# A decode block with its gradients: two weight gradients stored in blocks of 120 and 32 rows from another queue, and the side work in another order

## The chip, the cores and the metric

The kernel runs on one core of a Trainium2 chip. The metric is the device time of one execution in microseconds. The kernel before takes 1714.44 us, the median of three runs (1713.85 to 1715.55). The profiled execution spans 1712.4 us from its first to its last instruction.

## What is computed

A transformer block for one decode step, forward and backward. The batch is B = 4, the width D = 512, there are H = 32 heads of Dh = 128, the cache has Sk = 4096 rows, and the inner width of the feed-forward part is F = 1792. All data are bf16.

```python
def attn(x, K, V, wq, wo):                     # x: (4, 1, 512); K, V: (4, 32, 4096, 128)
    q = (x @ wq).reshape(B, 1, H, Dh).transpose(0, 2, 1, 3)
    p = softmax(einsum("bhqd,bhkd->bhqk", q, K) * Dh ** -0.5)
    o = einsum("bhqk,bhkd->bhqd", p, V)
    return o.transpose(0, 2, 1, 3).reshape(B, 1, H * Dh) @ wo

h  = x + attn(layernorm(x), K, V, wq, wo)
h2 = h + (silu(layernorm(h) @ w1) * (layernorm(h) @ w3)) @ w2

# returned: h2 and, for the given grad_out, the gradients of x, K, V, wq, wo, w1, w3, w2
```

The caches dominate. K and V hold 128 pairs of batch and head, 1 MB each; both are read, V is read a second time in the backward part, and the gradients of K and V, of the same size, are written. The gradients of wq (512 x 4096) and wo (4096 x 512) have 4 MB each, those of w1, w3 and w2 1.75 MB each.

## The kernel before

SBUF is cut into 23 slots of 128 partitions x 4160 bf16. A tile takes a slot, and gives it back when it has been used; who takes it next waits until the last reader is done, a store included.

The backward part goes through the 128 pairs, called heads here and in the code's index `s`. For each it loads V once more (a DMA issued by ACT), transposes it (TensorE and ACT), makes dP from it, and builds two outer products on VectorE, `gv` and `gk`, which are the gradients of V and K. The store of `gv` is issued by GpSimd, that of `gk` by SyncE.

```python
def grad_V(s):
    gv = Slot("gv")
    outer(gv.heads(), P2s.pop(s), reps["rdo", ...])          # VectorE
    nc.gpsimd.dma_start(out=rows_of(out_3[b, h]), in_=gv.heads())
    gv.give()

def grad_K(s):
    gk = Slot("gk")
    outer(gk.heads(), dS2s[s // B][:, s % B], reps["rq", ...])
    nc.sync.dma_start(out=rows_of(out_2[b, h]), in_=gk.heads())
    gk.give()
```

All else that the backward part has to do is a generator, `side_work`, whose units are run between the heads. A unit ends at a `yield`.

```python
def grad_unit(dst, lhsT, rhs):                   # one 128 x 512 piece of a weight gradient
    ps = psg.tile([P, 512], FP32)
    nc.tensor.matmul(ps[:, 0:n], lhsT=lhsT, rhs=rhs, start=True, stop=True)   # K = 4 rows
    grad_flush()                                 # ACT copies the piece before this one
    gu.append((dst, ps, n))

def side_work():
    ...
    for s in range(NH):                          # dq: 128 products in fp32, three to a unit
        nc.tensor.matmul(dq_ps[:, s:s + 1], lhsT=M_of(s)[:, 0:Dh], rhs=dOT_f[:, s:s + 1], ...)
        if s % MC == MC - 1:
            Ms[s // MC].give()
            if s // MC in (3, 5):
                load_wq2(s // MC // 2 - 1)       # wq once more, from SyncE
        if s % 3 == 2:
            yield
    ...                                          # dq to rows (dqflat)
    for cc in range(DC):                         # dx: wq transposed, 16 times 8 blocks, and multiplied
        for h0 in range(0, H, 8):
            ...                                  # 8 transposes
            yield
            nc.scalar.copy(out=wv[:, h0:h0 + 8, :], in_=pt[:])
        ...                                      # 3 more units
    ...                                          # layer norm backward, out_1
    for cc in range(DC):                         # gradient of wq: four blocks of 128 rows
        if cc == DC - 2:
            w2 = load_w2()
        st = Slot("gwq")
        for n8 in range(HD // 512):
            grad_unit(...)
            yield
        grad_flush()
        nc.gpsimd.dma_start(out=out_4[cc * P:(cc + 1) * P, :], in_=st.b(HD))
        st.give()
    ...                                          # rows for the feed-forward part, out_0
    ...                                          # gradient of w2 (14 units, 2 stores)
    ...                                          # oflat: the rows of O, by four small DMAs
    ...                                          # gradients of w1 and w3 (32 units, 4 stores)
    ...                                          # gradient of wo (32 units, 4 stores of 128 partitions)

for s in range(NH):                              # the loop over the heads
    load_ahead(s + L)
    ...
    front(s + L)                                 # V transposed, dP
    grad_V(s + LV)
    grad_K(s)
    ...
    if s >= S0:                                  # S0 = 21, L = 5, LV = 3
        step("s", 3 if s < S0 + 15 else 2)
    elif s >= O0:
        step("o")
step("s", 400)                                   # what is left
```

Of the kernel before, what the change touches and what calls it, by code (L numbers as in the profile page):

```python
# [24 lines left out]
def kernel(  # L25
# [22 lines left out]
    nc = tc.nc  # L48
    P = nc.NUM_PARTITIONS

    B = A_x.shape[0]
    D = A_x.shape[-1]
    H = A_k_cache.shape[1]
    Sk = A_k_cache.shape[2]
    Dh = A_k_cache.shape[3]
    F = B_w1.shape[1]
    NH = B * H
    HD = H * Dh
    assert NH == P and Dh == P and H == 32 and Sk == 32 * P
    assert D == 4 * P and F % P == 0  # L60
    DC = D // P
# [5 lines left out]
    MC = 16  # L67
# [110 lines left out]
    def ones_window(col):  # L178
# [11 lines left out]
                          in_=rowg[:, None, :, None].to_broadcast([P, 4, 8, 4]))  # L190
# [70 lines left out]
    with ExitStack() as c0:  # L261
# [11 lines left out]
        for h in range(H):  # L273
            for cc in range(DC):
                nc.tensor.matmul(qT_ps[:, h, :], lhsT=wq_s[cc].b(HD)[:, h * Dh:(h + 1) * Dh], rhs=xhatT[:, cc, :],
                                 start=(cc == 0), stop=(cc == DC - 1))
# [4 lines left out]
        for r in range(2):  # L281
            for t_ in range(2):
                for q in range(4):
                    nc.tensor.matmul(qr_ps[32 * q:32 * (q + 1), 2 * r + t_, :], lhsT=ident_b[:, 64 * r + t_:64 * (r + 1):2],
                                     rhs=qT_bf[:], start=True, stop=True, tile_position=(0, 32 * q))
# [5 lines left out]
    def M_of(s):  # L291
        return Ms[s // MC].f(MC * (Dh + 1)).rearrange("p (n c) -> p n c", c=Dh + 1)[:, s % MC, :]
# [206 lines left out]
    def load_w2():  # L499
        sl = two_slots("w2")  # L500
        for i in range(2):
            nc.sync.dma_start(out=sl[i].b(7 * D).rearrange("p (c j) -> p c j", c=7),
                              in_=B_w2.rearrange("(p c) j -> p c j", c=FC)[:, i * 7:(i + 1) * 7, :])
        return sl
# [92 lines left out]

    units = {"d": d_hh_units()}

    def step(k, n=1):  # L600
        for _ in range(n):
            next(units[k], None)

    for s in range(VQ):
        load_V(s)
# [108 lines left out]
    O_sb = pers2.tile([NH, Dh], BF16, name="O_sb")  # L714
# [85 lines left out]
    with ExitStack() as cm:  # L800
# [33 lines left out]
        for wi, wt in enumerate((w1, w3)):  # L834
            for fc in range(FC):
                for cc in range(DC):
                    nc.tensor.matmul(gu_ps[:, wi, fc, :], lhsT=w13_view(wt, cc)[:, fc * P:(fc + 1) * P], rhs=hhatT[:, cc, :],
                                     start=(cc == 0), stop=(cc == DC - 1))
# [25 lines left out]
        for jj in range(DC):  # L864
            i_mm = 0
            for (lt, wt) in ((d_gateT_bf, w1), (d_upT_bf, w3)):
                for fc in range(FC):
                    nc.tensor.matmul(dn_ps[:, jj, :], lhsT=w13_view(wt, jj)[:, fc * P:(fc + 1) * P], rhs=lt[:, fc, :],
                                     start=(i_mm == 0), stop=(i_mm == 2 * FC - 1))
# [3 lines left out]
        rs = Slot("reps")  # L873
        rep_bufs = {nm_: [rs.b()[:, (2 * k + i) * 512:(2 * k + i + 1) * 512].rearrange("p (i d) -> p i d", i=REP) for i in range(2)]
                    for k, nm_ in enumerate(("rq", "rdo"))}
        dh = rs.f(2080)[0:B, 1024:1024 + D]
# [3 lines left out]
        ps = psA.tile([P, REP, Dh], FP32, tag="rT", name="repq_ps")  # L880
# [4 lines left out]
        for s in range(3):  # L885
# [8 lines left out]
                         start=True, stop=True)  # L894
# [14 lines left out]
        for b0, b1 in ((0, 1), (1, B)):  # L909
            ps = psA.tile([P, B, Dh], FP32, tag="rT", name="rep_ps")  # L910
            for b in range(b0, b1):
                for jj in range(DC):
                    nc.tensor.matmul(ps[:, b, :], lhsT=dhT[:, jj, b:b + 1].to_broadcast([P, P]), rhs=wo_page(0)[:, 0, jj, :],
                                     start=(jj == 0), stop=(jj == DC - 1))
# [12 lines left out]
    with ExitStack() as c2:  # L927
# [7 lines left out]
        gu = []  # L935

        def grad_flush():
            if gu:
                dst, ps, n = gu.pop()
                nc.scalar.copy(out=dst, in_=ps[:, 0:n])  # L940


        def grad_unit(dst, lhsT, rhs):
            n = rhs.shape[-1]
            ps = psg.tile([P, 512], FP32, tag="gps", name="gps")
            nc.tensor.matmul(ps[:, 0:n], lhsT=lhsT, rhs=rhs, start=True, stop=True)  # L946
            grad_flush()
            gu.append((dst, ps, n))


        def side_work():
# [6 lines left out]
            def load_wq2(cc):  # L958
                if cc < DC:
                    wq2s.append(Slot("wq2"))  # L960
                    nc.sync.dma_start(out=wq2s[-1].b(HD), in_=A_wq[cc * P:(cc + 1) * P, :])

            for s in range(NH):
                nc.tensor.matmul(dq_ps[:, s:s + 1], lhsT=M_of(s)[:, 0:Dh], rhs=dOT_f[:, s:s + 1], start=True, stop=True)
                if s % MC == MC - 1:
                    Ms[s // MC].give()
                    if s // MC in (3, 5):
                        load_wq2(s // MC // 2 - 1)
                if s % 3 == 2:
                    yield  # L970
            yield
# [4 lines left out]
            pt = psg.tile([P, P], BF16, tag="gps", name="pt_dq")  # L976
            nc.tensor.transpose(pt[:], dqT_bf[:], ident_b[:])
            nc.scalar.copy(out=dqr_bf[:], in_=pt[:])
            flat = Slot("dqflat")
            yield  # L980
            for b in range(B):
                nc.gpsimd.dma_start(out=flat.b(HD)[b:b + 1, :], in_=dqr_bf[b::B, :])
            yield
# [3 lines left out]
            for cc in range(DC):  # L987
                wq2 = wq2s.popleft()
                wv = wq2.b(HD).rearrange("p (n c) -> p n c", c=P)
                for h0 in range(0, H, 8):  # L990
                    pt = psg.tile([P, 8, P], BF16, tag="gps", name="pt_wq")
                    for i in range(8):
                        nc.tensor.transpose(pt[:, i, :], wv[:, h0 + i, :], ident_b[:])
                    yield
                    nc.scalar.copy(out=wv[:, h0:h0 + 8, :], in_=pt[:])
                yield
                for h in range(H):
                    nc.tensor.matmul(dx_ps[0:B, cc * P:(cc + 1) * P], lhsT=dqT_bf[:, h * B:(h + 1) * B], rhs=wv[:, h, :],
                                     start=(h == 0), stop=(h == H - 1))
                    if h == H // 2 - 1:  # L1000
                        yield
                wq2.give()
                load_wq2(cc + 2)
                yield
# [3 lines left out]
            xhat_bf = fs.t[0:B, 6 * D:7 * D]  # L1008
# [5 lines left out]
            nc.vector.tensor_tensor(out=dx_bf, in0=dh, in1=lnbx, op=ALU.add)  # L1014
            nc.gpsimd.dma_start(out=o1_2, in_=dx_bf)
            yield
            for cc in range(DC):
                if cc == DC - 2:
                    w2 = load_w2()
                st = Slot("gwq")  # L1020
                for n8 in range(HD // 512):
                    grad_unit(st.b(HD)[:, n8 * 512:(n8 + 1) * 512], xhat_bf[0:B, cc * P:(cc + 1) * P],
                              flat.b(HD)[0:B, n8 * 512:(n8 + 1) * 512])
                    yield
                grad_flush()
                nc.gpsimd.dma_start(out=out_4[cc * P:(cc + 1) * P, :], in_=st.b(HD))
                st.give()
            flat.give()
            fs.give()

            r1, r2 = Slot("rows1"), Slot("rows2")
            hh_rows, dg_rows, du_rows = r1.t[0:B, 0:F], r1.t[0:B, F:2 * F], r2.t[0:B, 0:F]
            gr_bf, dh_bf, hhat_bf = r1.t[0:B, 2 * F:2 * F + D], r2.t[0:B, F:F + D], r2.t[0:B, F + D:F + 2 * D]
            nc.gpsimd.dma_start(out=gr_bf, in_=g2)
            nc.gpsimd.tensor_copy(out=dh_bf, in_=dh)
            nc.vector.tensor_scalar(out=hhat_bf, in0=hrows, scalar1=mv_h[:, 0:1], scalar2=rstd_h[:],
                                    op0=ALU.subtract, op1=ALU.mult)
            for dst_rows, srcT in ((hh_rows, hhT_bf), (dg_rows, d_gateT_bf), (du_rows, d_upT_bf)):
# [20 lines left out]
            nc.vector.tensor_tensor(out=h2_bf, in0=hrows, in1=o2_ps[0:B, :], op=ALU.add)  # L1059
            nc.gpsimd.dma_start(out=o0_2, in_=h2_bf)  # L1060
            yield
            for i in range(2):
                st = Slot("gw2")
                hw = hh_rows[:, i * 7 * P:(i + 1) * 7 * P].rearrange("b (p k) -> b k p", k=7)
                for k in range(7):
                    grad_unit(st.b(7 * D)[:, k * D:(k + 1) * D], hw[:, k, :], gr_bf)
                    yield
                grad_flush()
                nc.gpsimd.dma_start(out=out_8[i * 7 * P:(i + 1) * 7 * P, :].rearrange("(p c) j -> p c j", c=7),
                                  in_=st.b(7 * D).rearrange("p (c j) -> p c j", c=7))  # L1070
                st.give()
            oflat = Slot("oflat")
            for b in range(B):
                nc.gpsimd.dma_start(out=oflat.b(HD)[b:b + 1, :], in_=O_sb[b::B, :])
            for (rows, out_ap) in ((dg_rows, out_6), (du_rows, out_7)):
                for i in range(2):
                    st = Slot("gw13")
                    nw = hhat_bf[0:B, i * 2 * P:(i + 1) * 2 * P].rearrange("b (p k) -> b k p", k=2)
                    for k in range(2):
                        for (f0_, w_) in f_chunks:  # L1080
# [4 lines left out]
                    nc.gpsimd.dma_start(out=out_ap[i * 2 * P:(i + 1) * 2 * P, :].rearrange("(p c) f -> p c f", c=2),  # L1085
                                      in_=st.b(2 * F).rearrange("p (c f) -> p c f", c=2))
                    st.give()
            r1.give()
            for h0 in range(0, H, 8):
                st = Slot("gwo")  # L1090
                ow = oflat.b(HD)[0:B, h0 * P:(h0 + 8) * P].rearrange("b (p k) -> b k p", k=8)
                for k in range(8):
                    grad_unit(st.b(8 * D)[:, k * D:(k + 1) * D], ow[:, k, :], dh_bf)
                    yield
                grad_flush()
                nc.gpsimd.dma_start(out=out_5[h0 * P:(h0 + 8) * P, :].rearrange("(p k) j -> p k j", k=8),
                                  in_=st.b(8 * D).rearrange("p (k j) -> p k j", k=8))
                st.give()
            oflat.give()
            r2.give()  # L1100

        units["s"] = side_work()
# [106 lines left out]
        O0, S0, L, LV = 2, 21, 5, 3  # L1209

        def load_ahead(s):
            prefetch()
            if s < NH and s not in V2s and s not in VTs:
                load_V2(nc.scalar)
# [12 lines left out]
        for s in range(NH):  # L1227
            load_ahead(s + L)
            if s % REP == 0 and s + REP < NH:
                replicate(s + REP)  # L1230
            P_pairs(s + L)
            if s + L < NH:
                front(s + L)
            elif s + L == NH:
                rows_out()
                rows_T()
            if s > 0 and s + LV < NH:
                grad_V(s + LV)
            grad_K(s)
            if s % B == B - 1 and s + 1 < NH:  # L1240
                group_dS((s + 1) // B)
            if s >= S0:
                step("s", 3 if s < S0 + 15 else 2)
            elif s >= O0:
                step("o")
        step("s", 400)
# [30 lines left out]
```

## Time and profile before

| what | value |
|---|---|
| time, median of 3 | 1714.44 us |
| span of the profiled execution | 1712.4 us |
| busy: PE, DVE, ACT, POOL | 74%, 72%, 57%, 28% |
| moved by DMA | 707.49 MB, 413 GB/s on average |
| clock granted to TensorE, mean | 0.871 of full speed |
| DVE waits for a gv store before it builds a gv | 123.6 us in 42 waits |

PE is TensorE's matmuls, DVE VectorE, ACT ScalarE, POOL GpSimd and SP SyncE. The page cuts the span in 40 equal slices and gives for each the busy share of an engine in tenths, the mean busy share of the core's sixteen DMA engines, and what they moved in GB/s. A DMA queue belongs to the engine that issues: q1 holds what SP issues, q10 what ACT issues, q0 what POOL issues. "To landing" is the time from the issue of a transfer to its completion. The windows of the trace give busy times of any stretch, in the order PE, PEld (weight loads), DVE, ACT, POOL, clock, DMA share, GB/s; the figure in brackets counts instructions. In a group of waits stand the total, the number of waits and the longest.

### The profile page before, as it was taken

The page shows a single profiled execution, that of the slowest core. Times are in us where ns is not written, and L with a number is a line of the kernel's source. Part 1 is how long each engine was busy: PE and PEld are TensorE (multiplying, and loading weights), DVE is VectorE, ACT ScalarE, POOL GpSimd, SP SyncE. Part 2 cuts the span into 40 slices and gives each one's busy share as a digit, 9 for nine tenths or more (in the row PEclk, how much of TensorE's full clock was granted, in tenths as well). Part 3 has the DMA queues.
Part 4 walks back from the last instruction along what each step waited for, and adds up shares of the span by engine and source line. Part 5 has one row for each costly group of instructions (what it writes and reads, how often), then busy time and mean ns, then how long its engine had stood idle before and what let it go on. Part 6 is the DMA issues. An engine that isn't in the chain of part 4 may idle for free. (4 is left out here: it accounts for less than half of the span.)

```text
span 1712.4 us, 38306 instructions
## 1 busy us (share of the span) xinstructions
PE 1259.2 (74%) x16180; PEld 930.6 (54%) x16180; DVE 1229.2 (72%) x1294; ACT 969.7 (57%) x1502; POOL 474.7 (28%) x822
## 2 busy tenths in 40 slices
PE   5889888888888888776788986675657656656660
PEld 4767677677677666644556764443334433333330
DVE  5989999989998996466667548475546465656584
ACT  3556445444544444676655466675766656666660
POOL 1211232223222321122333245353223231211140
PEclk8999999999999999898776579887896788887885
DMA  9999999999999999799999999999999999999997
GB/s 401 424 424 424 424 424 424 424 420 424 419 424 407 420 407 401 307 385 423 425 425 426 426 365 422 425 424 425 425 426 426 424 417 418 424 425 423 425 424 299
DMA packets 101740, 707.49 MB, mean 413 GB/s; under 512 B 11052, under 2 KB 15288, under 8 KB 17600
## 3 DMA queue, kind: packets, MB, share of 16 engines
q1 hardware_dynamic: 63568, 432.04, 60.5%
q0 software_dynamic: 20864, 148.22, 20.7%
q10 hardware_dynamic: 17136, 124.79, 17.6%
q8 instruction: 127, 2.08, 0.5%
q14 instruction: 45, 0.37, 0.1%
HBM read 422.59 MB, written 282.34 MB: 412 GB/s over the span
## 5 line engine op out<-in xcount | busy, mean ns | idle before, releaser
L765 ACT COPY V<-pt_tps 128x1024 bf16<-128x1024 bf16 x512 | 490.8, 1025 | 155.3 <-PE pt_tps L764 115.9
L764 PE MATMUL pt_tps<-ident_b,V 128*128 128x128 bf16 x4096 | 359.0, 249 | 206.5 <-ACT V L765 201.4
L764 PEld LDWEIGHTS <-V 128*128 128x128 bf16 x4096 | 306.8, 114 | 269.1 <-issue 257.8
L770 DVE TENSOR_TENSOR gv<-P,reps 128x4096 bf16<-128x4096 bf16 x125 | 287.0, 2296 | 129.4 <-DMA out_dram<-gv 123.6
L770 DVE TENSOR_TENSOR gk<-dS,reps 128x4096 bf16<-128x4096 bf16 x128 | 292.5, 2287 | 112.7 <-DMA out_dram<-gv 80.4
L421 DVE TENSOR_TENSOR PK<-Kn,PK 128x4096 bf16<-128x4096 bf16 x128 | 292.4, 2284 | 26.4 <-POOL PK L417 26.0
L436 PE MATMUL M_ps<-PK,Vn 128*128 128x130 bf16 x4096 | 285.8, 222 | 32.3 <-DMA Vn<-in_A_v_cache_dram 31.9
L436 PEld LDWEIGHTS <-Vn 128*128 128x128 bf16 x4096 | 253.8, 99 | 52.0 <-DMA Vn<-in_A_v_cache_dram 43.0
L328 DVE STREAM_TRANSPOSE KT<-Kn 128x512 f32<-128x512 f32 (+1 forms) x321 | 250.7, 797 | 0.3 <-issue 0.2
L1177 PE MATMUL dP_ps<-V,zd 128*32 128x512 bf16 x1024 | 185.3, 452 | 72.3 <-ACT V L765 61.8
L323 ACT COPY KT<-pt_tps 128x1024 bf16<-128x1024 bf16 x128 | 129.5, 1012 | 185.3 <-PE pt_tps L322 150.7
L781 POOL DMA_DIRECT2D out_dram<-gv x128 | 68.4, 535 | 498.9 <-DVE gv L770 470.6
L417 POOL COPY PK<-P_all 128x64 bf16<-128x64 bf16 x128 | 32.6, 255 | 415.5 <-ACT P_all L411 412.4
L334 POOL TENSOR_TENSOR W<-qrep,wmask 128x128 bf16<-128x128 bf16 x128 | 122.9, 960 | 83.0 <-PE S_ps L354 68.3
L1147 POOL COPY P<-P_all 128x64 bf16<-128x64 bf16 x127 | 137.3, 1081 | 0.0
L1177 PEld LDWEIGHTS <-zd 128*32 128x32 bf16 x1024 | 37.3, 96 | 161.8 <-issue 140.3
L1142 POOL COPY zd<-dOT_bf 128x2 bf16<-128x2 bf16 x128 | 90.5, 708 | 71.5 <-PE dP_ps L1177 71.5
L1191 DVE TENSOR_SCALAR dPr<-dPT_ps,c_rep 128x32 f32<-128x32 f32 x128 | 23.2, 242 | 119.1 <-PE dPT_ps L1159 118.9
L1131 ACT CAST reps<-rep_ps 128x512 bf16<-128x512 f32 x62 | 36.4, 586 | 121.0 <-DVE gk L770 86.5
L411 ACT COPY P_all<-pt_P 32x64 bf16<-32x64 bf16 x256 | 52.1, 203 | 53.8 <-PE pt_P L407 51.6
L322 PE MATMUL pt_tps<-ident_b,Kn 128*128 128x128 bf16 x1024 | 81.0, 224 | 0.0
L446 PE MATMUL kP_ps<-PK,onesw 128*32 128x512 bf16 x1024 | 79.9, 389 | 0.0
(244 smaller groups left out, 1358.7 us busy)
## 6 DMA issues: line engine op xcount, KB each, us to landing
Kn<-in_A_k_cache_dram SPq DMA_DIRECT2D x128, 1024.0 KB, 15.3
Vn<-in_A_v_cache_dram SPq DMA_DIRECT2D x128, 1024.0 KB, 15.6
out_dram<-gv POOLq DMA_DIRECT2D x128, 1024.0 KB, 29.7
out_dram<-gk SPq DMA_DIRECT2D x128, 1024.0 KB, 13.9
V<-in_A_v_cache_dram ACTq DMA_DIRECT2D x119, 1024.0 KB, 14.8
V<-in_A_v_cache_dram SPq DMA_DIRECT2D x9, 1024.0 KB, 18.3
wq<-in_A_wq_dram SPq DMA_DIRECT2D x8, 1024.0 KB, 18.3
out_dram<-gw POOLq DMA_DIRECT2D x6, 896.0 KB, 42.0
```

What stands on the lines that cost most here:

```text
L322: nc.tensor.transpose(pt[:, i, :], Kn[:, c * GW + i, :], ident_b[:])
L323: nc.scalar.copy(out=KT[:, c * GW:(c + 1) * GW, :], in_=pt[:])
L328: nc.vector.transpose(out=KT[:, c * w_:(c + n) * w_], in_=Kn[:, c * w_:(c + n) * w_])
L334: nc.gpsimd.tensor_tensor(out=W[:, hl], in0=qrep[:, :, s:s + 1].to_broadcast([P, 4, 32]), in1=wmask[:, hl, None, :].to_broadcast([P, 4, 32 ...
L421: nc.vector.tensor_tensor(out=PK[:, :, 0:Dh].rearrange("p j (r t) -> p j r t", t=2), in0=Ks[s].heads().rearrange("p j (r t) -> p j r t", t=2),
L436: nc.tensor.matmul(hold["M"][:], lhsT=Vn[:, j, :], rhs=PK[:, j, :], start=(j == 0), stop=(j == SJ - 1))
L764: nc.tensor.transpose(pt[:, i, :], v[:, g * GW + i, :], ident_b[:])
L765: nc.scalar.copy(out=v[:, g * GW:(g + 1) * GW, :], in_=pt[:])
L770: nc.vector.tensor_tensor(out=dst.rearrange("p j (r t) -> p j r t", t=2), in0=col2[:, :, None, :].to_broadcast([P, SJ, Dh // 2, 2]), in1=r ...
L1142: nc.gpsimd.tensor_copy(out=zd[s % B][:, 32:132:67], in_=dOT_bf[:, s:s + 1].to_broadcast([P, 2]))
L1147: nc.gpsimd.tensor_copy(out=P2s[s][:], in_=P_all[:, s, :, None].to_broadcast([P, SJ, 2]))
L1177: nc.tensor.matmul(rows["acc"][32 * c:32 * (c + 1), :], lhsT=zq_window(zd[hl], 2 * hl + u), rhs=VT[:, j0:j0 + 4, :], start=(hl == 0 and u ...
```

## The change

Three things are done together.

First, the gradients of wq and wo are no longer stored in four blocks of 128 rows (for wo, of 128 partitions with 8 rows each) from GpSimd, but in four blocks of 120 and one of 32, from SyncE. For each block the same eight pieces are computed, with 120 or 32 rows.

Second, the order of the side work: the gradient of wo comes right after dq and before dx, and no longer last; its rows (`oflat`) are prepared within the dq stage. The second load of wq is started within the blocks of wo, no longer within dq. The gradients of w1 and w3 come ahead of that of w2. `dh_bf`, a small cast, goes from GpSimd to VectorE.

Third, the pace. A head now gets 2.4 units of side work from head 21 on; before it was 3 for fifteen heads and 2 after them. A unit of the transposes of wq counts as 1.5.

The aim is to spread the side work evenly over the heads and to put these stores elsewhere than in GpSimd's queue. The core of the diff (the moves of whole loops are cut):

```diff
+    credit = {}
     def step(k, n=1):
-        for _ in range(n):
-            next(units[k], None)
+        credit[k] = credit.get(k, 0) + n
+        while credit[k] > 0:
+            credit[k] -= next(units[k], None) or 1
...
         def grad_unit(dst, lhsT, rhs):
-            nc.tensor.matmul(ps[:, 0:n], lhsT=lhsT, rhs=rhs, start=True, stop=True)
+            nc.tensor.matmul(ps[0:m_, 0:n], lhsT=lhsT, rhs=rhs, start=True, stop=True)
+        row_blocks = [(r0, min(r0 + 120, 512)) for r0 in range(0, 512, 120)]
...
                     Ms[s // MC].give()
-                    if s // MC in (3, 5):
-                        load_wq2(s // MC // 2 - 1)
+                    if s // MC == 6:
+                        oflat = Slot("oflat")
+                        for b in range(B):
+                            nc.gpsimd.dma_start(out=oflat.b(HD)[b:b + 1, :], in_=O_sb[b::B, :])
...
+            yield
+            dh_bf = rs.t[0:B, 3328:3328 + D]
+            nc.vector.tensor_copy(out=dh_bf, in_=dh)
+            for (r0, r1_) in row_blocks:
+                st = Slot("gwo")
+                ow = oflat.b(HD)[0:B, r0 * 8:r1_ * 8].rearrange("b (p k) -> b k p", k=8)
+                for k in range(8):
+                    grad_unit(st.b(8 * D)[:, k * D:(k + 1) * D], ow[:, k, :], dh_bf)
+                    yield
+                grad_flush()
+                nc.sync.dma_start(out=out_5[r0 * 8:r1_ * 8, :].rearrange("(p k) j -> p k j", k=8),
+                                  in_=st.b(8 * D)[0:r1_ - r0].rearrange("p (k j) -> p k j", k=8))
+                st.give()
+                if r0 in (240, 360):
+                    load_wq2(r0 // 120 - 2)
...
-                    yield
+                    yield 1.5
                     nc.scalar.copy(out=wv[:, h0:h0 + 8, :], in_=pt[:])
...
-            for cc in range(DC):
-                if cc == DC - 2:
+            for (r0, r1_) in row_blocks:
+                if r0 == 240:
                     w2 = load_w2()
                 st = Slot("gwq")
...
-                nc.gpsimd.dma_start(out=out_4[cc * P:(cc + 1) * P, :], in_=st.b(HD))
+                nc.sync.dma_start(out=out_4[r0:r1_, :], in_=st.b(HD)[0:r1_ - r0])
...
-                step("s", 3 if s < S0 + 15 else 2)
+                step("s", 2.4)
```

More of the change, by code (lines that the diff above doesn't have):

```diff
@@ L938, in grad_flush @@
             if gu:
-                dst, ps, n = gu.pop()
-                nc.scalar.copy(out=dst, in_=ps[:, 0:n])
+                dst, ps = gu.pop()
+                nc.scalar.copy(out=dst, in_=ps)
         def grad_unit(dst, lhsT, rhs):
-            n = rhs.shape[-1]
+            n, m_ = rhs.shape[-1], lhsT.shape[-1]
             ps = psg.tile([P, 512], FP32, tag="gps", name="gps")
-            nc.tensor.matmul(ps[:, 0:n], lhsT=lhsT, rhs=rhs, start=True, stop=True)
+            nc.tensor.matmul(ps[0:m_, 0:n], lhsT=lhsT, rhs=rhs, start=True, stop=True)
             grad_flush()
-            gu.append((dst, ps, n))
+            gu.append((dst[0:m_], ps[0:m_, 0:n]))
+        row_blocks = [(r0, min(r0 + 120, 512)) for r0 in range(0, 512, 120)]
         def side_work():
@@ L978, in side_work @@
             nc.scalar.copy(out=dqr_bf[:], in_=pt[:])
+            yield
[13 more added lines that the diff above has]
+                    load_wq2(r0 // 120 - 2)
+            oflat.give()
             flat = Slot("dqflat")
-            yield
             for b in range(B):
@@ L993, in side_work @@
                         nc.tensor.transpose(pt[:, i, :], wv[:, h0 + i, :], ident_b[:])
-                    yield
+                    yield 1.5
                     nc.scalar.copy(out=wv[:, h0:h0 + 8, :], in_=pt[:])
@@ L1021, in side_work @@
                 for n8 in range(HD // 512):
-                    grad_unit(st.b(HD)[:, n8 * 512:(n8 + 1) * 512], xhat_bf[0:B, cc * P:(cc + 1) * P],
+                    grad_unit(st.b(HD)[:, n8 * 512:(n8 + 1) * 512], xhat_bf[0:B, r0:r1_],
                               flat.b(HD)[0:B, n8 * 512:(n8 + 1) * 512])
@@ L1032, in side_work @@
             hh_rows, dg_rows, du_rows = r1.t[0:B, 0:F], r1.t[0:B, F:2 * F], r2.t[0:B, 0:F]
-            gr_bf, dh_bf, hhat_bf = r1.t[0:B, 2 * F:2 * F + D], r2.t[0:B, F:F + D], r2.t[0:B, F + D:F + 2 * D]
+            gr_bf, hhat_bf = r1.t[0:B, 2 * F:2 * F + D], r2.t[0:B, F + D:F + 2 * D]
             nc.gpsimd.dma_start(out=gr_bf, in_=g2)
-            nc.gpsimd.tensor_copy(out=dh_bf, in_=dh)
             nc.vector.tensor_scalar(out=hhat_bf, in0=hrows, scalar1=mv_h[:, 0:1], scalar2=rstd_h[:],
@@ L1061, in side_work @@
             yield
[L1062 to L1074, printed above, removed]
             for (rows, out_ap) in ((dg_rows, out_6), (du_rows, out_7)):
@@ L1087, in side_work @@
                     st.give()
[L1088 to L1093, printed above, removed]
+            for i in range(2):
+                st = Slot("gw2")
+                hw = hh_rows[:, i * 7 * P:(i + 1) * 7 * P].rearrange("b (p k) -> b k p", k=7)
+                for k in range(7):
+                    grad_unit(st.b(7 * D)[:, k * D:(k + 1) * D], hw[:, k, :], gr_bf)
                     yield
                 grad_flush()
-                nc.gpsimd.dma_start(out=out_5[h0 * P:(h0 + 8) * P, :].rearrange("(p k) j -> p k j", k=8),
-                                  in_=st.b(8 * D).rearrange("p (k j) -> p k j", k=8))
+                nc.gpsimd.dma_start(out=out_8[i * 7 * P:(i + 1) * 7 * P, :].rearrange("(p c) j -> p c j", c=7),
+                                  in_=st.b(7 * D).rearrange("p (c j) -> p c j", c=7))
                 st.give()
-            oflat.give()
+            r1.give()
             r2.give()
```

## The prediction

> **What bounds the kernel now.** I read the page's 40 slices first, then its DMA queues, then the same quantities by stage, and last the chain of work that ended last.
>
> ```profile
> DMA  9999999999999999799999999999999999999997
> GB/s 401 424 424 424 424 424 424 424 420 424 419 424 407 420 407 401 307 385 423 425 425 426 426 365 422 425 424 425 425 426 426 424 417 418 424 425 423 425 424 299
> ...
> q1 hardware_dynamic: 63568, 432.04, 60.5%
> q0 software_dynamic: 20864, 148.22, 20.7%
> q10 hardware_dynamic: 17136, 124.79, 17.6%
> ```
>
> All but two slices are nines: the sixteen DMA engines are full, at about 425 GB/s. 707.49 MB at 425 GB/s is 1664.7 us. The span is 1712.4 us, so 47.7 us is DMA time lost in slices under 425. An engine that computes can gain nothing unless it fills such a hole. The holes, in the windows of the trace: about 18 us between 645 and 774 us, where the forward part ends and the backward part starts (280 GB/s in 688 to 731), which the diff doesn't touch; some 7 us at the start and in the forward part, untouched; and the two below.
>
> ```profile
> core 0: us, PE busy (x) PEld busy (x) DVE busy (x) ACT busy (x) POOL busy (x), PEclk, DMA share, GB/s
> 880.00:1000.00 120.00, 107.07 (x827) 85.49 (x824) 66.95 (x47) 58.42 (x65) 36.70 (x42) 0.63 1.01 425
> 1000.00:1024.00 24.00, 17.28 (x192) 11.83 (x191) 19.14 (x14) 17.98 (x21) 17.98 (x18) 0.91 0.84 320
> 1024.00:1240.00 216.00, 142.35 (x1471) 94.41 (x1471) 136.40 (x103) 146.09 (x178) 87.12 (x86) 0.84 1.01 424
> ...
> 1677.00:1687.00 10.00, 0.00 (x0) 0.00 (x0) 9.97 (x9) 0.00 (x0) 0.53 (x1) 0.50 1.01 424
> 1687.00:1697.00 10.00, 0.00 (x0) 0.00 (x0) 1.89 (x1) 0.00 (x0) 0.00 (x0) 0.50 1.01 426
> 1697.00:1707.00 10.00, 0.00 (x0) 0.00 (x0) 0.00 (x0) 0.00 (x0) 0.00 (x0) 0.50 0.26 111
> 1707.00:1712.40 5.40, 0.00 (x0) 0.00 (x0) 0.00 (x0) 0.00 (x0) 0.00 (x0) 0.50 0.03 12
> ```
>
> **The dip:** 24 us at 320 GB/s after 1000 us lose 24 x (1 - 320/425) = 5.9 us. It follows 120 us in which PE was busy for 107 (89%) at a clock of 0.63 while DVE had 67. That is the dq stage of the side work; the DMA queues lived on their backlog until it was gone. **The tail:** the queues are full until 1697 us; then 15.4 us carry only 111 x 10 + 12 x 5.4 = 1.17 MB, which takes 2.8 us at full rate.
>
> Who still moves bytes in that tail? The trace records sixteen completions for each transfer, one for each DMA engine. For the last gv store (issued at 1680.4) fifteen of them come between 1687.3 and 1697.0, the sixteenth at 1709.9. For the last gk store (1688.9) fifteen come between 1696.8 and 1702.2, the sixteenth at 1708.1. **One of the sixteen engines is late**, and the program ends with it. On the gv stores the gap between fifteenth and sixteenth is 0.1 us at 1040 us, 2 at 1240, 7 at 1280, 11 at 1400, 14 at 1440 and 12 to 17 from there to the end. The issue table shows the same from afar:
>
> ```profile
> out_dram<-gv POOLq DMA_DIRECT2D x128, 1024.0 KB, 29.7
> out_dram<-gk SPq DMA_DIRECT2D x128, 1024.0 KB, 13.9
> out_dram<-gwq POOLq DMA_DIRECT2D x4, 1024.0 KB, 28.2
> out_dram<-gwo POOLq DMA_DIRECT2D x4, 1024.0 KB, 48.0
> ```
>
> The stores have one size; those from POOL land 2 to 3.5 times later, those of gwo at 48 us. The chain (DMA out_dram<-gv, 20% of the span, on the page) is this same wait.
>
> [...] So 128 rows use sixteen, 120 rows fifteen, and 32 rows sixteen with two rows each; the trace of before has only sixteens for its large transfers and can't confirm the fifteen. [...] The trace agrees that one engine lags, and only since POOL's queue is in use (in the forward part the last two completions are 0.1 to 0.2 us apart); it doesn't number it. [...] gk's last two completions mostly lie 0.5 us apart.
>
> **The change, part by part.**
>
> 1. Block sizes. A gradient of wq or wo has 4 MB; an 8 KB row goes to one engine. Before: four stores of 128 rows, 8 rows an engine, 4 x 64 = 256 KB on each of sixteen. After: four of 120 rows on fifteen engines, 8 rows each, and one of 32 rows, 2 each: 272 KB on fifteen and 16 KB on the sixteenth. Both gradients together: the sixteenth is relieved of 480 KB, the rest get 32 KB more. q1 moved 432.04 MB in 60.5% of 16 x 1712.4 = 16,576 engine-us: 26.1 KB a us. So 480 KB is 18.8 us of the sixteenth engine, and 32 KB is 1.3 us of the others. The lag at the end is 13 us: the relief is larger than the lag, if the late engine is the sixteenth.
> 2. What the tail can give. The sixteen completions of the last gk store average 1699.9. With all even, the last data land near 1700, plus the 2.4 us from the last completion to the end of the span: 1702.5, a gain of 10 us at most. It won't be all: the wo stores come early (below), when there is no lag to pay off, and an engine that is ahead can store only what is queued for it. After the wq stores, gw13 and gw2 still go out in 128s from POOL, and before's lag grew to 14 us between 1240 and 1440. I take 6 us, between 2 and 10.
> 3. Pacing. The side work before has 196 units; 15 heads x 3 and then 2 a head end it at head 111. After: 16 more units for ten blocks instead of eight, 8 more for the 16 transposes that now count 1.5, in all 220; 220/2.4 = 92 heads, head 112. The end doesn't move. The dq stage has 42 units: 14 heads before, 17.5 after.
> 4. The dip. In the dq stage dq itself held PE for 36.09 us (the windows of that tile alone):
>
> ```profile
> 880.00:1000.00 120.00, 36.09 (x235) 34.96 (x234) 0.00 (x0) 0.63 1.01 425
> ```
>
>    14 gv stores were issued in those 120 us, 8.57 us a head, PE busy 7.65, of it 2.58 for dq. At 2.4 instead of 3 units dq is 2.06, PE 7.13, and at the same busy share of 89% a head takes 8.0 us. DMA needs 3.146 MB / 425 = 7.4 us a head. So PE still falls behind, 0.6 us a head over 17.5 heads, 10.5 us; before, 1.17 x 14 = 16.4 us, less 4.9 us for the two wq loads that filled in. Net 11.5 before and 10.5 after (the loads now come within the wo stage): the backlog that absorbed 5.6 of it before absorbs as much again, and the dip shrinks by 1 us only. If the clock rises with less load it shrinks more. I take 2 us, 0 to 5.
> 5. The queue. Ten stores go to SP instead of eight to POOL; an issue costs POOL 0.53 us (the tile's own row), 4.3 us in all, and POOL is busy for 28% of the span: nothing. But POOL stood still before such a store, and the gv stores behind it:
>
> ```profile
> POOL out_dram L1026 <- ACT gwq L940: 44.1, 4, 16.6
> ```
>
>    Now SP stands still instead, and gk stores behind it. q0 falls by 8.4 MB and q1 rises by it. Stage 1240 to 1480 runs at 423: 1 us to gain there from gv slots that come free sooner.
> 6. The order, the cast of dh on DVE (one small instruction), the early oflat: off the path, 0.
>
> Sum: 6 + 2 + 1 = 9 us: 1714.4 - 9 = 1705.
>
> **The rivals.** (a) The late engine isn't the one that 120 rows leave out. Then it gets 1.3 us more, and the tail grows by about that: 1713 to 1716. For it: no view numbers engines. Against it: [...] nothing else explains a block of 120. (b) The whole lag goes and the slower dq pace removes the dip: 10 + 5 + 1 = 16 us, 1698. For it: the lag of 13 is under the relief of 18.8. Against it: the dq balance in 4, and relief that comes too early. (c) The new order opens a hole: SP waits for ACT up to 16.6 us ahead of each store, or the 2.4 units in the later heads (2 before) make PE and ACT the bound. Against it: in 1240 to 1480 PE is busy 63% and ACT 64%; 0.4 units more a head is 0.17 us of PE and 0.24 us of ACT. It would cost 3 to 6 us, 1709 or so with the tail gained. (d) Transfers hidden anyway: nothing moves, 1714.
>
> **Range and chances.** Tail 2 to 10, dip 0 to 5, holes -4 to 1: 1696 to 1713. 2% is 34 us, near the whole of what is lost to DMA, so neither outer chance is worth more than 1 in 100.
>
> **What will show it.** The last gv and gk stores: fifteenth and sixteenth completion within 5 us of each other (step 2); the slices' last figure over 299. The stores of gwq and gwo: landing under 20 us (step 5). The dq stage: PE still near 89% busy, and a dip after it that is less than 6 us deep (step 4). It is wrong if the sixteenth completion still trails by 13 us, if the dip widens because the wq loads no longer fill it, or if a stage that ran at 424 falls below 415.

## The result, and the profile after

The changed kernel takes 1738.57 us (median of 4 runs, 1737.43 to 1739.62), against 1714.51 us: a ratio of 1.014, with a 95% interval of 1.0122 to 1.0157. I had predicted 1705 us and a range up to 1713. The change makes the kernel 24 us slower.

The page of the kernel after, its slices and its queues:

```profile
DMA  9999999999999999799999999999999999999998
GB/s 401 424 424 424 425 423 424 424 421 424 419 423 408 415 408 400 267 424 423 423 425 425 425 420 405 375 374 383 420 394 417 380 395 380 413 408 424 425 426 347
...
q1 hardware_dynamic: 64744, 440.43, 61.7%
q0 software_dynamic: 19712, 139.83, 19.5%
```

The busy row is as full of nines as before. The row under it isn't: between the 26th and the 34th slice there are figures of 374 to 395 where before had 417 to 426. The engines are busy and move less. The windows show it by stage (columns as before: PE, PEld, DVE, ACT, POOL, clock, DMA share, GB/s):

```profile
880.00:1000.00 120.00, 102.42 (x869) 79.30 (x870) 78.37 (x54) 64.13 (x72) 42.29 (x53) 0.73 1.01 425
1000.00:1024.00 24.00, 20.50 (x157) 15.55 (x157) 11.55 (x14) 13.02 (x16) 6.10 (x8) 0.64 1.01 422
1024.00:1240.00 216.00, 135.22 (x1218) 92.98 (x1218) 117.97 (x81) 130.74 (x164) 73.25 (x79) 0.76 0.99 390
1240.00:1480.00 240.00, 146.65 (x1426) 96.46 (x1426) 137.24 (x105) 150.89 (x188) 77.72 (x86) 0.80 1.00 396
1480.00:1677.00 197.00, 130.78 (x1234) 79.28 (x1232) 120.18 (x82) 136.91 (x177) 60.06 (x82) 0.85 1.01 419
...
1720.00:1737.80 17.80, 0.00 (x0) 0.00 (x0) 0.00 (x0) 0.00 (x0) 0.00 (x0) 0.50 0.55 234
```

In the kernel before, two of these stages read:

```profile
1240.00:1480.00 240.00, 150.74 (x1384) 93.88 (x1382) 139.41 (x100) 153.82 (x197) 66.33 (x100) 0.80 1.01 423
1480.00:1677.00 197.00, 122.89 (x1152) 75.01 (x1151) 130.01 (x87) 125.64 (x156) 45.88 (x82) 0.84 1.01 424
```

The loss of a stage is its length times (1 - rate/425). The dip after dq is gone: 422 where before had 320, a gain of 5.7 us. The tail carries 234 x 17.8 = 4.17 MB, which takes 9.8 us at full rate, so it loses 8.0 us; before lost 12.6, a gain of 4.6 us. But the three stages from 1024 to 1677 now lose 17.8, 16.4 and 2.8 us, where before (424, 423, 424) lost 0.5, 1.1 and 0.5: 34.9 us more. 34.9 - 5.7 - 4.6 = 24.6, which is the measured slowdown within its uncertainty. So the question is why DMA moves 390 to 396 GB/s in just the two stages in which the blocks of 120 rows are stored.

The issue table of the kernel after:

```profile
out_dram<-gv POOLq DMA_DIRECT2D x128, 1024.0 KB, 20.6
out_dram<-gk SPq DMA_DIRECT2D x128, 1024.0 KB, 22.5
...
out_dram<-gwo SPq DMA_DIRECT2D x4, 960.0 KB, 30.0
out_dram<-gwq SPq DMA_DIRECT2D x4, 960.0 KB, 30.0
```

gv lands sooner than before (20.6 against 29.7 us), gk later (22.5 against 13.9), and the blocks of 960 KB take 30.0 us. The backlog changed queues. In the sixteen completions of each of these blocks the first stands 0.5 us after the issue and the others at 7 to 38 us; the earliest completion of any gv or gk store, here and in the kernel before, stands at 3.7 us. The packets of SyncE's queue say the same: 6760 of them have 4 bytes, for 423 transfers, eight short of sixteen for each, and there are eight such blocks (before: 6608 for 413, sixteen for each). One of them ends an engine's part of a transfer: at the end of the kernel before, where from 1702.3 to 1709.5 us the DMA share is 0.06, one engine of sixteen, eight packets of 8 KB of SyncE's queue stand between two of 4 bytes (1702.8 and 1707.7 us). So **fifteen engines carry a block of 120**, eight rows each on average, and all sixteen one of 32 (its first completions come at 4.4 and 5.2 us).

The packets, the pieces of a transfer that the trace records one by one, say what is slow. Packets of 8 KB carry 97% of the bytes; their usual time, the median, is 309 ns. In the records of the trace after 700 us:

| kernel | mean of an 8 KB packet | share over 400 ns |
|---|---|---|
| before | 312.7 ns | 0.95% |
| after | 321.1 ns | 3.00% |

Between 1360 and 1460 us the packets of SyncE's queue take 371 ns on average and a tenth of them 568 ns or more, nearly twice the usual; those of the gv stores beside them, in GpSimd's queue, take 336 ns. Averaged over the sixteen engines, the time above 310 ns is 37.4 us an engine after, 11.2 before. These 26 us are the larger part of the 34.9; the rest are holes (DMA share 0.90 to 0.93 in three stretches of 20 us).

### The profile page after: what moved, and what is told of

The parts are those of the page before. It is cut to its first block, busy times and chain, and to the rows that moved or that the text cites. A ratio compares the mean times of both kernels' runs of the same rounds, so it can differ in the third digit from the quotient of the medians.

```text
span 1737.8 us, 38364 instructions
## 1 busy us (share of the span) xinstructions
PE 1269.2 (73%) x16196; PEld 943.1 (54%) x16196; DVE 1228.9 (71%) x1295; ACT 977.5 (56%) x1518; POOL 489.7 (28%) x813
## 5 line engine op out<-in xcount | busy, mean ns | idle before, releaser
L1154 POOL COPY P<-P_all 128x64 bf16<-128x64 bf16 x127 | 155.3, 1223 | 0.0
L1184 PEld LDWEIGHTS <-zd 128*32 128x32 bf16 x1024 | 37.4, 96 | 157.6 <-issue 142.5
## 6 DMA issues: line engine op xcount, KB each, us to landing
out_dram<-gv POOLq DMA_DIRECT2D x128, 1024.0 KB, 20.6
out_dram<-gk SPq DMA_DIRECT2D x128, 1024.0 KB, 22.5
```

Source lines behind the costliest of these rows:

```text
L1154: nc.gpsimd.tensor_copy(out=P2s[s][:], in_=P_all[:, s, :, None].to_broadcast([P, SJ, 2]))
L1184: nc.tensor.matmul(rows["acc"][32 * c:32 * (c + 1), :], lhsT=zq_window(zd[hl], 2 * hl + u), rhs=VT[:, j0:j0 + 4, :], start=(hl == 0 and u ...
```

## The experiments

Theory 1: the shape of the blocks slows the DMA engines. Theory 2: the new order and pace starve the queues. Theory 3: the stores in SyncE's queue hold up gk. The change has three parts, so I ran the corners between before and after.

**New order and pace, SyncE, blocks of 128.**

```diff
-        row_blocks = [(r0, min(r0 + 120, 512)) for r0 in range(0, 512, 120)]
+        row_blocks = [(r0, r0 + 128) for r0 in range(0, 512, 128)]
```

> New order and pace, stores from SyncE, but in blocks of 128 rows. Theory 1 (the 120-row shape slows the DMA engines while such a store is in flight): the stretches at 375 to 397 GB/s go back to 424, about 34 us come back, and the dip and part of the tail stay gained: 1696 to 1708 us. Theory 2 (order and pace starve the DMA queues): stays at 1730 to 1740. Theory 3 (SyncE, held up by these stores, delays gk): 1730 to 1740 too.

Measured: 1717.5 us, 1.0014 of before (1.0003 to 1.0026). 21 us of the 24 come back with the block height alone; theory 2 is refuted, and theory 3 as the main cause. The stretches with the stores run at full rate again, in the windows of this kernel:

```profile
1030.00:1160.00 130.00, 85.15 (x733) 55.23 (x731) 66.20 (x48) 79.91 (x101) 36.14 (x53) 0.71 1.01 423
1300.00:1480.00 180.00, 114.11 (x1074) 69.63 (x1073) 106.15 (x77) 120.28 (x157) 55.51 (x70) 0.81 1.01 423
```

and in the same windows of the kernel after:

```profile
1030.00:1160.00 130.00, 83.10 (x648) 55.23 (x649) 66.95 (x44) 76.93 (x100) 41.48 (x47) 0.71 1.00 394
1300.00:1480.00 180.00, 108.83 (x984) 69.90 (x982) 102.74 (x80) 111.76 (x144) 58.47 (x65) 0.76 1.01 394
```

The reader should look at the last two columns together: share 1.0 with 394 GB/s means busy engines and slow packets (321.1 ns on average after 700 us, against 312.7 before); a share under 1 would mean engines that stand idle. But this kernel isn't under the range I gave, 1696 to 1708. It has holes of the second sort, about 10 us in 1180 to 1280 us (where two slices show 377 and 360).

**New order and pace alone: blocks of 128 from GpSimd.**

```diff
-                nc.sync.dma_start(out=out_5[...], ...)
+                nc.gpsimd.dma_start(out=out_5[...], ...)         # out_4 likewise
```

> New order and pace alone: blocks of 128 rows from GpSimd as before. Theory 1: no slow stretch; the dip after dq is gone (about -6 us) and the tail with its late engine stays: 1704 to 1712. Theory 2: 1730 to 1740. Theory 3: like theory 1, and clearly faster than the same kernel with the stores from SyncE.

Measured: 1713.45 us, 0.9987 (0.998 to 0.9993). It is the only version that beats both kernels, by 0.13%. The dip after dq is gone (418 GB/s in 1000 to 1024 us) and yet hardly anything is left of its 5.9 us. Two things took it. In GpSimd's queue one engine is late, as in the kernel before, and later still: the sixteenth completion of the last gv stores trails the fifteenth by 18 to 22 us instead of 13 to 15. And there is a new hole:

```profile
1380.00:1420.00 40.00, 22.55 (x224) 14.41 (x224) 28.97 (x24) 22.28 (x28) 18.25 (x18) 0.79 0.94 381
```

It loses 40 x (1 - 381/425) = 4.1 us. In the waits of this stretch VectorE stands still for gv and gwq stores to land, for up to 5.3 us, because the slot that it wants is held until the last of the sixteen completions:

```profile
DVE gk L773 <- DMA out_dram<-gv: 8.5, 2, 5.3
...
DVE rows L1057 <- DMA out_dram<-gv: 5.1, 1, 5.1
DVE gk L773 <- DMA out_dram<-gwq: 4.6, 1, 4.6
```

**New order and pace, blocks of 120 and 32, from GpSimd.** The edit above on the changed kernel, which keeps its blocks.

> New order and pace, blocks of 120 and 32 rows, but from GpSimd. Theory 1 in its narrow form (the spread over fifteen engines that SyncE's queue makes is the cause): fast, 1700 to 1712, with packets of 310 ns. In its wide form (any store of 120 rows): 1730 to 1740. Theory 3: fast.

Measured: 1734.28 us, 1.0107 (1.0079 to 1.0136). The wide form holds: it isn't the queue. The first of the sixteen completions stands at 4.5 to 29 us here, none at 0.5: that one is seen in SyncE's queue alone. The packets are as slow (319.8 ns, 2.95% over 400). Two engines are late in this kernel: the last gv store has fourteen completions within 10.3 us, and the others at 27.1 and 29.4.

**Order and pace of before, blocks of 120 and 32 from SyncE.** The new `row_blocks`, `grad_unit` and stores, put into the kernel before.

> Order and pace of before, only the blocks of 120 and 32 rows from SyncE. Theory 1: the loss moves with the stores: GB/s under 400 in about 1130 to 1260 and in 1480 to 1600, some 30 us slower than before, 1738 to 1750. Theory 2: no loss, 1705 to 1715. If the late engine of before is the one left out by 120 rows, its lag on gv stores (12 to 17 us at the end) shrinks.

Measured: 1732.95 us, 1.011 (1.0086 to 1.0133), a smaller loss than the 30 us or so that I had expected. It moves with the stores. The windows of this kernel around the wq blocks and the wo blocks, which the old order puts last:

```profile
1140.00:1330.00 190.00, 114.00 (x998) 71.50 (x996) 97.75 (x72) 112.51 (x143) 48.41 (x69) 0.74 1.00 395
1540.00:1700.00 160.00, 101.25 (x869) 65.34 (x868) 105.55 (x76) 100.19 (x127) 48.78 (x60) 0.79 1.01 399
```

The kernel before has 426 and 422 there:

```profile
1140.00:1330.00 190.00, 127.55 (x1143) 79.11 (x1141) 112.00 (x79) 126.89 (x161) 64.97 (x85) 0.79 1.01 426
1540.00:1700.00 160.00, 84.67 (x811) 51.88 (x810) 105.99 (x70) 86.10 (x104) 35.01 (x57) 0.79 1.00 422
```

Does this run tell **which engine is late**? While the five wo blocks are stored, between 1548 and 1676 us, the gap between the fifteenth and sixteenth completion of the gv stores falls from 12.4 us (median of those issued in 1520 to 1560) to 7.9, 5.5 and 1.7 in the next three stretches of 40 us; in the kernel before it stays at 12 to 17 there. That fits a late engine which 120 rows leave out, but it doesn't show it. With blocks of 128 from SyncE in the same order ("The queue alone", below) no engine is left out (64,720 packets in SyncE's queue, 1152 more than before: 128 and sixteen for each of the eight blocks), and the gap falls in the same stretches from 23.9 us to 18.2, 18.2 and 12.7. So taking the stores out of GpSimd's queue may be what shrinks it. Blocks of 120 in GpSimd's queue, the run above, don't remove the lag, but no record says whether they leave an engine out there, or which. Rival (a) of the prediction stays open.

**Only wq in blocks of 120.** In the changed kernel the wo loop takes blocks of 128.

> As the changed kernel, but the gradient of wo in blocks of 128; only that of wq in 120 and 32. Theory 1, both forms: half the loss, 1724 to 1731; the stretch 1030 to 1160 us runs at 424 GB/s, and the one with the wq stores (1300 to 1480) at 380 to 400. If the loss were of the order or of the queue: 1735 or 1717, and no such split.

Measured: 1729.69 us, 1.0083 (1.0066 to 1.01). The split within one run is as expected: 424 GB/s with the wo blocks of 128, 388 with the wq blocks of 120 (there the share is 0.98, so a part of that loss is idle engines).

```profile
1030.00:1160.00 130.00, 83.59 (x796) 53.51 (x797) 74.10 (x52) 86.66 (x110) 45.10 (x54) 0.82 1.01 424
1300.00:1480.00 180.00, 105.27 (x969) 64.86 (x968) 96.51 (x69) 108.62 (x140) 61.79 (x62) 0.79 0.98 388
```

The remaining question was what it is about 120 rows: one engine left out (1a), or any height that isn't 128 (1b).

**Blocks of 112 and 64 rows.** 120 becomes 112 throughout; again five blocks and forty units.

> As the changed kernel, with blocks of 112, 112, 112, 112 and 64 rows instead of 120 and 32: again five blocks and forty units, from SyncE[...]. Theory 1a (what costs is that one engine is left out and the others are loaded unevenly): like blocks of 128, 1714 to 1722, packets of 8 KB mean 313 ns after 700 us. Theory 1b (what costs is the layout[...]): 1732 to 1745, mean packet 318 ns or more, and all sixteen completions of the store after several us, none at 0.5.

Measured: 1742.52 us, 1.0156 (1.0135 to 1.0176). No engine is left out (completions of a block from 3.9 us on, none at 0.5; SyncE's queue has 64,752 packets, eight more than in the changed kernel), and it is as slow as the changed kernel: packets of 319.6 ns, 2.54% over 400. Theory 1a falls.

**Blocks of 128, stored as two transfers of 64 partitions.**

```diff
-                nc.sync.dma_start(out=out_4[r0:r1_, :], in_=st.b(HD)[0:r1_ - r0])
+                for p0 in (0, 64):
+                    nc.sync.dma_start(out=out_4[r0 + p0:r0 + p0 + 64, :], in_=st.b(HD)[p0:p0 + 64])
```

> Blocks of 128 rows computed as one, but stored as two transfers of 64 partitions each from SyncE. Everything else as with one transfer of 128 (1717.5 us). Theory 1a: unchanged, 1714 to 1721. Theory 1b: slow, 1730 to 1745, with a share of packets over 400 ns near 3% instead of 1%.

Measured: 1734.24 us, 1.0132 (1.0086 to 1.0178); packets 319.8 ns, 2.84% over 400. The blocks are computed as in the run with 128 from SyncE (1717.5 us); the shape of the store alone makes the 17 us. Its windows:

```profile
1030.00:1160.00 130.00, 72.82 (x651) 46.41 (x648) 65.72 (x43) 75.14 (x96) 37.18 (x51) 0.77 1.01 397
1300.00:1480.00 180.00, 119.00 (x1016) 75.93 (x1016) 106.89 (x72) 114.75 (x148) 56.60 (x67) 0.74 1.01 403
```

**Eight transfers of 16 partitions.** The same with 16.

> The same blocks of 128 rows stored as eight transfers of 16 partitions each. [...] Theory 1a: 1716 to 1725 (only more issues on SyncE). Theory 1b: at least as slow as two of 64, 1735 to 1765, with the slowest packets longer than in any other run.

Measured: 1730.94 us, 1.0098 (1.0083 to 1.0113); packets 318.8 ns, 2.04% over 400, the longest 3021 ns against 2226 in the changed kernel. Slow as well, but not slower than two of 64: I had expected 1735 or more, so a dose doesn't follow from the height.

**Two transfers of 128 partitions with half rows.** The control: as many transfers as with 64, full height, 4 KB of each row.

> Control for the two transfers of 64 partitions: again two transfers of 512 KB for each block, from SyncE, but both are 128 partitions high and take half of each row (4 KB). If the height is what counts: like one transfer of 128, 1714 to 1722, packets over 400 ns near 1.1%. If smaller or more transfers on SyncE cost the time: 1730 to 1745 with near 3%.

Measured: 1719.76 us, 1.0022 (1.0012 to 1.0031); packets of 8 KB 314.1 ns, 1.32% over 400. Two transfers of half the size cost about 2 us; the height makes the rest. Its windows read 408 and 409 GB/s in the two stretches, but with a share of 0.99 and holes under 330 in single stretches of 20 us: idle engines, not slow packets. The deepest hole:

```profile
1420.00:1440.00 20.00, 15.93 (x137) 9.46 (x135) 16.63 (x13) 13.27 (x18) 15.21 (x12) 0.90 0.78 292
```

**The queue alone:** order and pace of before, blocks of 128, from SyncE.

> Order and pace of before, blocks of 128 rows, but from SyncE: the queue alone. If the queue doesn't matter: 1712 to 1717. If SyncE's in-order waits cost something, as 1717.5 against 1713.5 us under the new order may say: 1717 to 1722.

Measured: 1718.4 us, 1.0017 (1.0005 to 1.0028). The queue costs about 3 us, as 1717.5 against 1713.45 under the new order. SyncE's own waits fit that. In this run it stands for 206.5 us, in 33 waits, until a gk store has landed (the kernel before: 73.2); in the changed kernel:

```profile
SPq L1208 <- DMA out_dram<-gk: 239.2, 40, 17.4
...
SPq L996 <- ACT gwo L943: 36.5, 4, 12.6
```

SyncE now carries a backlog (gk lands after 23.2 us in this run and 22.5 in the changed kernel, against 13.9 before), and waits for blocks that aren't computed yet (the 36.5 us above). That these waits are the 3 us is argued, not shown.

**The pace alone:** the kernel before with 2.2 units a head.

```diff
-                step("s", 3 if s < S0 + 15 else 2)
+                step("s", 2.2)                       # with the credit of the change
```

> Before with the pace alone changed: 2.2 units a head from head 21 on (196 units, done at head 111 as before). If the dip after dq comes from 3 units a head: no dip (before: 320 GB/s for 24 us, 5.9 us lost), tail as before, 1708 to 1711. If another hole takes its place: 1713 to 1716.

Measured: 1716.27 us, 1.0006 (0.9993 to 1.0019), no difference. The dip moved:

```profile
1000.00:1024.00 24.00, 19.07 (x151) 15.13 (x147) 7.56 (x4) 10.58 (x12) 3.76 (x7) 0.61 1.01 427
1110.00:1150.00 40.00, 26.52 (x319) 19.78 (x319) 18.88 (x13) 26.20 (x30) 12.86 (x14) 0.90 0.89 358
```

It runs at 427 after dq, and loses 40 x (1 - 358/425) = 6.3 us around 1130 us.

The corners together (us; the kernel before had medians of 1714.5 to 1715.2 beside them):

| order and pace | 128, GpSimd | 128, SyncE | 120 and 32, GpSimd | 120 and 32, SyncE |
|---|---|---|---|---|
| old | 1714.5 | 1718.4 | not run | 1733.0 |
| new | 1713.5 | 1717.5 | 1734.3 | 1738.6 |

The blocks of 120 cost 21 us under the new order (in either queue) and 15 under the old; SyncE 3 to 4 with blocks of 128; the new order gains 1.

## Why the prediction was wrong

**Step 1, the block sizes: here it failed.** The count of engines was right (fifteen completions of a block of 120 at 7 to 38 us, one at 0.5). The 480 KB and 18.8 us of relief are an estimate that takes the left-out engine to be the same in all eight blocks; no run shows that, nor whether it is the late one. Wrong was the rate: I took 26.1 KB a us, that of transfers 128 partitions high, for transfers of another height. With such blocks a tenth of the packets in SyncE's queue takes 568 ns or more instead of 309 (1360 to 1460 us), and those in GpSimd's queue are slowed too (330 ns on average against 311). The stages that ran at 424 and 423 fell to 390 and 396, which the prediction had named as a sign of being wrong. 8 MB stored this way cost an engine 26 us of longer packets on average, to take, by that estimate, 18.8 us off one. I had a term for the transferred bytes and none for how they lie. The rivals missed it too: (c) held a hole opened by waits to cost 3 to 6 us, and none of the four had the DMA engines themselves slower.

Why the height matters isn't shown. What the runs show is that stores of 16, 64, 112 and 120 partitions are slow (1730.9 to 1742.5 us from SyncE under the new order, 8 KB packets of 318.8 to 321.1 ns) and stores of 128 in full or half rows are not (1717.5 and 1719.8 us; 314.1 ns with half rows). No record here names the engine of a packet or what held it up. Transfers of 16 partitions, for which I had expected more than two of 64, came out no slower (1730.9 against 1734.2 us). And no run here separates the end of the store in SBUF from the end in HBM.

**Step 2, the tail:** right in sign and nearly in size, but the relief isn't shown to be the cause. The fifteenth and sixteenth completion of the last gv store are 0.3 us apart instead of 13, and the tail gained 4.6 us where I took 6. Yet more than one engine trails: the last three completions come 26.5 to 28.8 us after the issue, the eighth at 18.0. And the last 17.8 us, 234 GB/s in the changed kernel and 122 in the kernel before, carry as much with half rows of 128 partitions from SyncE, which leave no engine out (65,872 packets in SyncE's queue, 2304 more than before: 128 and sixteen for each of the sixteen transfers; first line), though less with whole rows of 128 (second line):

```profile
1701.40:1719.20 17.80, 0.00 (x0) 0.00 (x0) 0.00 (x0) 0.00 (x0) 0.00 (x0) 0.50 0.56 238
1697.90:1715.70 17.80, 0.00 (x0) 0.00 (x0) 0.00 (x0) 0.00 (x0) 0.00 (x0) 0.50 0.34 145
```

So a full tail needs no relieved engine, and that this term came out near its size may be luck.

**Step 3, pacing:** nothing contradicts it; the end of the side work isn't where time was lost.

**Step 4, the dip:** the size was off, in the good direction: 5.7 us gained where I took 2. I had scaled PE's time a head at the old clock; the clock rose from 0.63 to 0.73 in the dq stage, as the text allowed for. But the gain there isn't one of the kernel: with the pace alone it comes back as a hole 110 us later, and in the new order with blocks of 128 as the hole at 1380. I had seen the dip as a place; these runs read as if it were a debt of the whole stage, paid where the backlog ends.

**Step 5, the queue:** wrong in size and sign. I gave the move to SyncE 1 us of gain; it costs 3 to 4. The landings of gwo and gwq that I put under 20 us are 30.0.

**Step 6** (cast, early oflat) shows nowhere in the losses, and wasn't tried by itself.

## What to carry to other kernels

Where a DMA-bound kernel stores large tiles, try first to keep the transfers 128 partitions high, even if one engine then lags: here the other heights tried cost 13 to 25 us under the new order (from SyncE), and the tail with its lag of 13 us lost 12.6. Loads weren't tried. Read the DMA share and the GB/s side by side: a full share with a low rate meant slow packets here (1.01 with 394 GB/s), a share under 1 idle engines (0.78 with 292), and they have different cures. An engine that lagged showed in two places here, at the end of the program (13 us) and in the buffers that wait for the last of sixteen completions (up to 5.3 us each in the hole at 1380); so look at all sixteen completions before shifting bytes (a small gap between the last two can also mean that two engines are late: 27.1 and 29.4 us above, with the other fourteen within 10.3), and ask what the new shape of the transfer does to the rate.

## What I had not expected of the hardware

A store of another height slows its neighbours. In the changed kernel the packets of GpSimd's queue, mostly gv stores of 128 partitions, take 330 ns on average while a gwo or gwq block is in flight, and 311 in the rest of the time after 700 us; with blocks of 128 from SyncE they take 311 in both. The V loads, in ACT's queue, don't show it: 321 ns while a block is in flight, 323 otherwise.

The lag of a late engine changes its queue. In the kernel before it was in GpSimd's (12 to 17 us at the end, SyncE's mostly under 1 from 1310 us until the last few stores). In the changed kernel, between 1120 and 1200 us, it was in SyncE's (12 to 17 us for most gk stores; a block of 32 rows issued at 1181 us has fifteen completions within 6.3 us and the last at 19.1), with GpSimd's gap at 0.3 to 2.6 from 1136 us on. There a loaded engine is the late one: in each block of 120 the last of the fifteen that carry it comes 2.4 to 7.4 us after the one before it. The late engine serves the two queues by turns: in the kernel before, from 1702.8 to 1706.1 us, its twelve packets of 8 KB come one by one, alternately from GpSimd's queue and from SyncE's, and each takes the usual 309 ns. Why one engine falls behind stays open; no run here was made for it.
